# Pooling of keys and values by halving additions in one tile, in an attention and mixture-of-experts kernel

## Chip, cores and metric

One core of a Trainium2 chip runs one program. Its engines are PE (matmuls), DVE (VectorE), ACT (ScalarE), POOL (GpSimd) and SP (which issues most DMAs). The metric is the device time of one execution in microseconds; the median of the runs counts.

## The reference

Three stages follow each other. The change lies in the first. Keys and values are averaged over eight neighbouring tokens before attention.

```python
B, H, S, D = q.shape            # 8, 8, 576, 64
k_p = k.reshape(B, H, S // 8, 8, D).mean(axis=3)
v_p = v.reshape(B, H, S // 8, 8, D).mean(axis=3)
scores = np.matmul(q, k_p.transpose(0, 1, 3, 2)) / np.sqrt(D)
attn = np.exp(scores - np.max(scores, axis=-1, keepdims=True))
attn = attn / (np.sum(attn, axis=-1, keepdims=True) + 1e-09)
x = np.matmul(attn, v_p)        # then [B * S, H * D] = [4608, 512]
```

The second stage picks one of eight experts for each of the 4608 rows (gate logits plus a bias of the row's modality) and applies the expert's two matrices with a ReLU between. The third applies `w_in`, h times softmax(h), a normalization and `w_out`.

## The kernel before

**Pooling.** Of a batch, the 8 heads times 72 pooled tokens are 576 rows of 8 x 64 numbers. They are cut into five row blocks of 128, 128, 128, 120 and 72 rows (`ROWS`), so there are 40 blocks, numbered 5 b + c. A block's keys are loaded as a tile `kc` of 512 columns, its values as `vc` (`load_kv`, L263 to L271), each from five buffers. DVE sums the keys over the eight tokens by one `tensor_reduce` whose input is read with a stride of 64 (`pool_k`, L301). The values of blocks 0 to 18 (`VD`, L45) are summed by DVE in the same way (L340), those of blocks 19 to 39 by POOL in three additions of halves, through the scratch tiles `v1` and `v2` (L343 to L347). Sums go to the tile `kv`, whose part 0 is keys and part 1 values.

**Around it.** Batch 0 has a path of its own (`first_keys`, L306): five key loads, the first queries, five value loads; its value sums are held behind its last keys (L350). Groups of two, two and one blocks then pass five steps: sums (`kv_a`), transposes on PE (`kv_b`, L359), copies on ACT (`kv_e`), gate products on PE (`kv_c`, L383) and, in `kv_d`, a mask product on POOL that spreads the values over heads (L399).

**Attention.** There are 20 units, five to a pair of batches; 36 row tiles in all. A unit's queries are transposed (`st_q`), scores are made in three banks (`st_s`), their maxima found on DVE (`st_m`, L466), exponentials on ACT (`st_x`), transposed (`st_e`), multiplied with the values (`st_v`, L545) and divided on DVE (`st_w`, L568 to L576); the rows are stored by SP (L577). After each nine tiles the rows are ranked by expert (`route`, `rank`) and POOL scatters them in nine indirect DMAs (`scatter`, L640). The first slot's expert weights are loaded and split when 18 tiles are scattered.

**Order.** The lists `ORDER` and `loads` (L779) give the program order of a step. The order on PE, ACT, DVE, POOL and SP is then set by the framework's scheduler, by program order and its own estimates of when an instruction is ready; each engine works through its queue in order. SP's queue holds key, value and query loads, row stores, weight loads, and, once, the loads of the modality table and the bias (L803 to L816). A load waits in it until a buffer of its tile is free.

**After attention.** The fixed weights `w_in` and `w_out` are decoded from 64-bit words on ACT, DVE (L188 to L208) and POOL (L195 to L209) beside the first two slots. From then on 19 slots of 256 rows pass through the experts and the third stage, with PE as the busy engine.

Of the kernel before, what the change touches and what calls it, by code (L numbers as in the profile page):

```python
# [7 lines left out]
F32 = mybir.dt.float32  # L8
# [29 lines left out]
# which groups of a unit's scores have their maximum taken off on VectorE  # L38
SUBG = ((2,),) * 20
# after which of the first values the second unit's queries are loaded  # L40
# [3 lines left out]
# the row blocks (five to a batch) whose values are pooled on VectorE, not GpSimd  # L44
VD = tuple(range(19))  # L45
Q0 = 3
LKV, LQ = 3, 5
# the first slot's loads, by steps since its expert was chosen
# [10 lines left out]
# a step's parts: what, which, and how many units ahead of the step  # L59
# [9 lines left out]
# the last pair's tiles that are routed together  # L69
# [10 lines left out]
def chunk_attention_moe_solu_kernel(  # L80
# [79 lines left out]
    def fixed_load(src, n, i, *_):  # L160
        kk, cc = divmod(i, n // 512)
        # before the first slot's exponentials their place serves too
        in_ec = (i if n > 512 else 8 + i) in EC
        st = ec_p.tile([128, FF], F32, name="ec") if in_ec else stg_p.tile([128, 1024], F32, name="stg")
        rows = src[128 * kk:128 * kk + 128, 512 * cc:512 * cc + 512]
        if src.dtype != I64:
            SY.dma_start(out=st[:, 0:512], in_=rows)
        else:
            SY.dma_start(out=st.bitcast(I32), in_=rows.bitcast(I32))
        return st  # L170

    def fixed_chunk(st, src, n, i, hi, lo, scale=None):
        """Chunk i (512 columns) of a [rows, n] weight, rows 128 to a partition block, as hi + lo."""
# [4 lines left out]
        if src.dtype != I64:  # L178
            t = st[:, 0:512]
        else:  # L180
            w = st.bitcast(I32).rearrange("p (f w) -> p f w", w=2)
            w0, w1_ = w[:, :, 0], w[:, :, 1]
            ta = dec_p[0].tile([128, 512], I32, name="ta")
            tb = dec_p[0].tile([128, 512], I32, name="tb")
            t, r = ta.bitcast(F32), tb.bitcast(F32)
            # the high word read as a float32 orders magnitudes too: below float32's range they become 0
            ACT.activation(out=t, in_=w1_.bitcast(F32), func=ACTF.Abs)
            DVE.tensor_scalar(out=t, in0=t, scalar1=2.0 ** -15, scalar2=None, op0=ALU.max)  # L188
            DVE.tensor_scalar(out=ta, in0=ta, scalar1=3, scalar2=0x3FFFFFFF, op0=ALU.logical_shift_left, op1=ALU.bitwise_and)
            DVE.scalar_tensor_tensor(out=ta, in0=w1_, scalar=-0x40000000, in1=ta, op0=ALU.bitwise_and, op1=ALU.bitwise_or)  # L190
            DVE.tensor_scalar(out=tb, in0=ta, scalar1=-0x800000, scalar2=None, op0=ALU.bitwise_and)
            ACT.activation(
                out=w0.bitcast(F32), in_=w0.bitcast(U32), func=ACTF.Copy, scale=2.0 ** -52 if sc is None else g52[:, kk:kk + 1])
            ic = i if n > 512 else 8 + i
            (DVE if ic in RD else POO).tensor_tensor(out=r, in0=w0.bitcast(F32), in1=r, op=ALU.mult)  # L195
# [15 lines left out]
    def expert_load(src, e, kk, n):  # L211
        """Rows of expert e's weight for n of its row blocks of 128, 1024 floats to a partition."""
        st = stg_p.tile([128, 1024], F32, name="stg")
        SY.dma_start(
            out=st.rearrange("p (k f) -> p k f", k=n),
            in_=src[bass.ds(e, 1), 128 * kk:128 * (kk + n), :].rearrange("a (k p) f -> p (a k) f", p=128))
        return st
# [6 lines left out]
    def behind(op, other):  # L224
        """Keeps op behind an earlier one of its engine."""
        tc.add_manual_dep(op.ins, other.ins.name, mybir.DependencyInfo(mybir.DependencyClass.NoSync, mybir.DependencyReason.DATA))
# [20 lines left out]
    t1_p = att0.enter_context(tc.tile_pool(name="t1_p", side="right", bufs=BUFS["t1"]))  # L247
# [11 lines left out]
    k_t, v_t, q_t = {}, {}, {}  # L259

    KVS = ((k, k_t, "kc"), (v, v_t, "vc"))

    def load_kv(b, c, which=KVS):  # L263
        a, z = ROWS[c]
        for src, dst, nm in which:
            t = kv_p.tile([128, POOL * D], F32, name=nm)
            SY.dma_start(
                out=t[:z - a],
                in_=src[b].rearrange("h (s t) d -> (h s) (t d)", t=POOL)[a:z],
            )  # L270
            dst[b, c] = t  # L271
# [26 lines left out]
    # a batch's pooled keys and values in three groups of its five row blocks  # L298
    KG = [(b, cs) for b in range(B) for cs in ((0, 1), (2, 3), (4,))]

    def pool_k(kv, kc, n):  # L301
        DVE.tensor_reduce(out=kv[:n, 0], in_=kc[:n].rearrange("p (t d) -> p d t", d=D), axis=AX.X, op=ALU.add)
# [3 lines left out]
    def first_keys():  # L306
        """The first batch's pooled keys, ahead of its values."""
        for c in range(5):
            load_kv(0, c, KVS[:1])
        load_q(0)  # L310
        for c in range(5):
            load_kv(0, c, KVS[1:])
            if c == Q1:
                load_q(1)
        for b, cs in KG[:3]:
            a0, z0 = ROWS[cs[0]][0], ROWS[cs[-1]][1]
            kt = pstr.tile([128, 512], F32, name="tr")
            for c in cs:
                a, z = ROWS[c]
                kv = kx_p.tile([128, 2, D], F32, name="kv")  # L320
                pool_k(kv, k_t.pop((b, c)), z - a)
# [6 lines left out]
    def kv_a(i):  # L328
        b, cs = KG[i]
        kv_st[i] = []  # L330
        for c in cs:
            n = ROWS[c][1] - ROWS[c][0]
            vc = v_t.pop((b, c))
            if b == 0:
                kv = kv_0[c]
            else:
                kv = kx_p.tile([128, 2, D], F32, name="kv")
                pool_k(kv, k_t.pop((b, c)), n)
            if 5 * b + c in VD:
                op = DVE.tensor_reduce(out=kv[:n, 1], in_=vc[:n].rearrange("p (t d) -> p d t", d=D), axis=AX.X, op=ALU.add)  # L340
            else:
                op = None
                v1 = t1_p.tile([128, 4 * D], F32, name="v1")  # L343
                v2 = t1_p.tile([128, 2 * D], F32, name="v2")
                POO.tensor_tensor(out=v1[:n], in0=vc[:n, 0:256], in1=vc[:n, 256:512], op=ALU.add)
                POO.tensor_tensor(out=v2[:n], in0=v1[:n, 0:128], in1=v1[:n, 128:256], op=ALU.add)
                POO.tensor_tensor(out=kv[:n, 1], in0=v2[:n, 0:64], in1=v2[:n, 64:128], op=ALU.add)  # L347
            if b == 0 and op is not None:
                # the keys are waited for first
                behind(op, kv_last[-1])  # L350
# [52 lines left out]
    # units: five per pair of batches (b, k0) (b, k1) (the last 64 tokens of both) (b+1, k0) (b+1, k1)  # L403
# [27 lines left out]
    # scores of a unit in three banks of (up to) six blocks of 72: block i is head i//n of row r = i%n  # L431
    # (in the unit of two batches' ends: head i)
# [89 lines left out]
    def group(i):  # L522
        """The tiles that are routed together: a pair of batches' nine, of the last pair five and four."""
# [4 lines left out]
    # heads' 73 columns follow each other over two banks: seven of them end at the first one's end  # L528
    def st_v(u, r):
# [5 lines left out]
        if not ps2 and s_done.get(NU - 1) == 3 and not any(x[0] == "s" for x in ps):  # L535
            # no more scores: their banks hold every other tile of the last units
# [70 lines left out]
    def rank():  # L607
# [8 lines left out]
        # row p of tile j: earlier rows of its tile, and all of the tiles before it  # L616
# [39 lines left out]
    def pick_first(dst, val, tmp, mx):  # L656
        """dst = one-hot of the first largest of val, over the last axis of 8."""
# [6 lines left out]
    def choose():  # L664
        """The expert with most tokens so far, of 18 tiles, has more than SLOT: its first two slots go first."""
# [48 lines left out]
    def take(pool, shape, dt, name):  # L714
        """A tile: a new one, or, in the last slot's two branches, the next of those that both hold."""
# [40 lines left out]
    # the first slot's first stages go between the last units' parts  # L756
    begun = [0]

    def early(*at):
        if at and begun[0] < len(EARLY) and at != EARLY[begun[0]]:  # L760
            return
        while begun[0] < 5 and (not at or begun[0] < len(EARLY) and EARLY[begun[0]] == at):
            i = begun[0]
            begun[0] += 1
            if i == 0:
                assert min(kv_n) == len(KG) and not k_t and not v_t
# [35 lines left out]
    def more_loads():  # L802
# [14 lines left out]
        # a row's place in xs and its token  # L817
# [114 lines left out]
    def tables(tp):  # L932
# [23 lines left out]
        # the expert that goes last: the one with fewest rows in its last slot  # L956
# [35 lines left out]
        # rows left from a slot's start; its first row; its expert (an empty slot has the first one's)  # L992
# [68 lines left out]
    def st_S(s, t, pf):  # L1061
        """Off with the mean; the sum of squares."""
# [7 lines left out]
    def st_R(s, t, n):  # L1070
        """Rows' scale: r / sqrt(r^2 mean(c^2) + 1e-6) with r = 1 / (sum + 1e-9)."""
# [7 lines left out]
        # 1 / sqrt: a first value from the bits, then Newton's steps  # L1079
# [51 lines left out]
    def switch_regs(s):  # L1131
        """Whether slot s needs another expert's weights, which, and its first row."""
# [16 lines left out]
    def switch_split(ce, sts, dh, dl, n, pool=(), after=()):  # L1149
        with tc.If(ce[0] == 1):  # L1150
            for i in range(4):
                ops = expert_split(sts[i], flat(dh[:, n * i:n * i + n]), flat(dl[:, n * i:n * i + n]), POO if i in pool else DVE)
                if i == 0:
                    # behind what the tensor engine waits for
# [22 lines left out]
    for s in range(NSTAT - 1):  # L1177
# [8 lines left out]
        if s > 1:  # L1186
            # behind what the tensor engine waits for
# [209 lines left out]
```

## Time and profile before

| | |
|---|---|
| median of three runs | 1095.69 us (1093.2 to 1097.76) |
| span of the profiled execution | 1114.2 us |
| PE, DVE, ACT, POOL busy | 1060.4, 573.9, 403.9, 218.2 us |
| mean granted clock of TensorE | 0.981 |

The profiled execution is one run under the hardware profiler; its own time is known as its span, 18.5 us above the median of the runs. Shares are of the span; the stages differ, so each is read in a window of its own. PE's busy time counts modelled ends of pipelined matmuls. A line number is that of the kernel before.

### The profile page before, as it was taken

The numbers are of one execution on the slowest core, as the hardware profiler recorded it, in microseconds if no ns is written. First come the engines' busy times: TensorE is split into PE (matmuls) and PEld (weight loads), VectorE is DVE, ScalarE is ACT, GpSimd is POOL, SyncE is SP. The second block draws the span as 40 slices with busy tenths as digits, with TensorE's granted clock in tenths as the row PEclk, the third lists the DMA queues.
The fourth block names the chain that finished last, engine by engine and source line by source line (L and its number), as shares of the span: only waits on it lengthen the run. The fifth ranks groups of instructions, "written<-read, shape, count | busy, mean of one in ns | idle before, by whom it ended". The sixth has DMA issues, their size and how long they took to land.

```text
span 1114.2 us, 18506 instructions
## 1 busy us (share of the span) xinstructions
PE 1060.4 (95%) x6961; PEld 963.0 (86%) x6961; DVE 573.9 (52%) x1460; ACT 403.9 (36%) x870; POOL 218.2 (20%) x284
## 2 busy tenths in 40 slices
PE   5898979789999999999999999999999999999997
PEld 4788868788889899898998989999898998989875
DVE  7986757899953434333444433434335343333254
ACT  3666657444522322222234222322234222222232
POOL 3147453453420101101013010100121011010001
PEclk8999989989999999999999999999999999999999
DMA  9887856332200101001033010101221010010000
GB/s 254 222 243 216 242 170 213 107 115 96 77 30 11 38 1 39 29 11 39 1 115 100 15 39 2 37 8 32 97 93 39 1 39 26 8 39 2 19 19 32
DMA packets 58960, 81.19 MB, mean 73 GB/s; under 512 B 16670, under 2 KB 33054, under 8 KB 58848
## 3 DMA queue, kind: packets, MB, share of 16 engines
q1 hardware_dynamic: 50608, 59.28, 17.7%
q0 software_dynamic: 7152, 19.46, 5.1%
q10 hardware_dynamic: 1088, 1.05, 0.4%
q8 instruction: 59, 0.97, 0.4%
q14 instruction: 53, 0.43, 0.1%
HBM read 59.37 MB, written 19.63 MB: 71 GB/s over the span
## 4 chain that ended last, share of the span: by engine, by line
PE 62%; issue 10%; DVE 1%; POOL 1%; another core or an unknown queue 0%; POOLq 0%; ACT 0%
PE ab L736 15%; PE ab L735 15%; PE ab L737 15%; PE h L736 5%; PE h L735 5%; PE h L737 5%; PE tr L1101 2%; PE tr L728 1%; POOL out_dram L1120 1%; DVE ta L208 0%; DVE hl L752 0%; DVE ec L1067 0%; DVE ec L1054 0%; DVE c L1077 0%
## 5 line engine op out<-in xcount | busy, mean ns | idle before, releaser
L1120 POOL DMA_INDIRECT out_dram<-o,ids x37 | 37.7, 1019 | 683.0 <-ACT o L1119 557.9
L735 PE MATMUL ab<-hh,w2h 128*128 128x256 f32 x576 | 165.9, 288 | 3.7 <-DVE rpf L626 3.7
L737 PE MATMUL ab<-hh,w2l 128*128 128x256 f32 x576 | 163.7, 284 | 0.0
L736 PE MATMUL ab<-hl,w2h 128*128 128x256 f32 x576 | 163.2, 283 | 0.5 <-DVE hl L752 0.5
L735 PE MATMUL ab<-xh,w1h 128*128 128x256 f32 x544 | 154.6, 284 | 2.9 <-DVE hl L752 1.8
L736 PE MATMUL ab<-xl,w1h 128*128 128x256 f32 x544 | 154.3, 284 | 0.0
L737 PE MATMUL ab<-xh,w1l 128*128 128x256 f32 x544 | 153.5, 282 | 0.0
L736 PE MATMUL h<-wil,yh 128*128 128x512 f32 x296 | 116.4, 393 | 1.9 <-POOL wil L202 1.9
L735 PE MATMUL h<-wih,yh 128*128 128x512 f32 x296 | 117.9, 398 | 0.1
L737 PE MATMUL h<-wih,yl 128*128 128x512 f32 x296 | 116.0, 392 | 0.0
L735 PEld LDWEIGHTS ab<-hh,w2h 128*128 128x128 f32 x576 | 109.9, 191 | 3.8 <-issue 3.8
L736 PEld LDWEIGHTS ab<-hl,w2h 128*128 128x128 f32 x576 | 110.0, 191 | 0.7 <-DVE hl L752 0.7
L737 PEld LDWEIGHTS ab<-hh,w2l 128*128 128x128 f32 x576 | 109.1, 189 | 0.0
L1053 ACT ACTIVATE ec<-h,c,ids 128x1024 f32<-128x1024 f32 x36 | 43.4, 1207 | 177.4 <-DVE c L1052 177.3
L735 PEld LDWEIGHTS ab<-xh,w1h 128*128 128x128 f32 x544 | 102.5, 188 | 4.4 <-DVE hl L752 2.0
L737 PEld LDWEIGHTS ab<-xh,w1l 128*128 128x128 f32 x544 | 104.0, 191 | 0.0
L736 PEld LDWEIGHTS ab<-xl,w1h 128*128 128x128 f32 x544 | 102.8, 189 | 0.8
L1051 DVE TENSOR_REDUCE c<-h 128x1 f32<-128x1024 f32 x37 | 45.3, 1224 | 111.2 <-PE h L737 111.2
L735 PE MATMUL ab<-woh,ch 128*128 128x512 f32 x256 | 99.7, 389 | 0.0
L737 PE MATMUL ab<-woh,cl 128*128 128x512 f32 x256 | 99.6, 389 | 0.0
L736 PE MATMUL ab<-wol,ch 128*128 128x512 f32 x256 | 99.6, 389 | 0.0
L752 DVE SCALAR_TENSOR_TENSOR hl<-ab,hh 128x512 fp32r<-128x512 f32 x68 | 46.9, 689 | 98.2 <-ACT hh L751 98.2
(279 smaller groups left out, 2048.2 us busy)
## 6 DMA issues: line engine op xcount, KB each, us to landing
stg<-in_moe_w_dram SPq DMA_DIRECT2D x24, 512.0 KB
xs<-xr SPq DMA_DIRECT2D x36, 256.0 KB
qc<-in_q_dram SPq DMA_DIRECT2D x16, 512.0 KB
kc<-in_k_dram SPq DMA_DIRECT2D x24, 256.0 KB
vc<-in_v_dram SPq DMA_DIRECT2D x24, 256.0 KB
stg<-in_moe_w_in_dram SPq DMA_DIRECT2D x4, 512.0 KB
ec<-in_moe_w_in_dram SPq DMA_DIRECT2D x4, 512.0 KB
ec<-in_moe_w_out_dram SPq DMA_DIRECT2D x4, 512.0 KB
```

The lines of the kernel that those rows point to most:

```text
L728: PE.transpose(out=p[:, kk, :], in_=x[:, 128 * kk:128 * kk + 128], identity=ident)
L735: PE.matmul(out=o, lhsT=hi, rhs=rhi, start=first, stop=False)
L736: PE.matmul(out=o, lhsT=hi, rhs=rlo, start=False, stop=False)
L737: PE.matmul(out=o, lhsT=lo, rhs=rhi, start=False, stop=last)
L752: b = DVE.scalar_tensor_tensor(out=hl[:, m:m + 2], in0=p, scalar=0.0, in1=hh[:, m:m + 2].bitcast(F32), op0=ALU.max, op1=ALU.subtract)
L1051: DVE.tensor_reduce(out=mx[:, c1], in_=pf, axis=AX.X, op=ALU.max)
L1053: ACT.activation(out=ec, in_=pf, func=ACTF.Exp, bias=nb[:, c1], scale=g[:, c1], accum_out=s1[:, c1])
L1101: PE.transpose(out=p[:, j, :], in_=c[:, f:f + 128], identity=ident)
L1120: sc = POO.indirect_dma_start(out=out, out_offset=bass.IndirectOffsetOnAxis(ap=d["tok"][t], axis=0), in_=o, in_offset=None, bounds_check=N ...
```

## The change

Keys and values of a block get one tile `kvc` of two parts from five buffers; each part has its own load. `pooled` sums the eight tokens by three additions, in place in that tile: columns 0 to 255 plus 256 to 511, then halves of that, then halves again into `kv`. From batch 1 on the additions take both parts at once (2 x 256, 2 x 128, 2 x 64 results). They run on DVE, except in the eleven blocks 9, 12, 15, ... 39, where they run on POOL, keys included. Batch 0 does its keys and its values separately, both on DVE. The strided sums and the scratch tiles `v1`, `v2` are gone. Comments are dropped too.

```diff
-VD = tuple(range(19))
+PV = tuple(range(9, 40, 3))
...
-    t1_p = att0.enter_context(tc.tile_pool(name="t1_p", side="right", bufs=BUFS["t1"]))
...
-    def load_kv(b, c, which=KVS):
+    def load_kv(b, c, which=(0, 1)):
         a, z = ROWS[c]
-        for src, dst, nm in which:
-            t = kv_p.tile([128, POOL * D], F32, name=nm)
+        if (b, c) not in kv_t:
+            kv_t[b, c] = kv_p.tile([128, 2, POOL * D], F32, name="kvc")
+        for i in which:
             SY.dma_start(
-                out=t[:z - a],
-                in_=src[b].rearrange("h (s t) d -> (h s) (t d)", t=POOL)[a:z],
+                out=kv_t[b, c][:z - a, i],
+                in_=(k, v)[i][b].rearrange("h (s t) d -> (h s) (t d)", t=POOL)[a:z],
             )
-            dst[b, c] = t
...
-    def pool_k(kv, kc, n):
-        DVE.tensor_reduce(out=kv[:n, 0], in_=kc[:n].rearrange("p (t d) -> p d t", d=D), axis=AX.X, op=ALU.add)
+    def pooled(eng, kv, t, i, n):
+        for w in (256, 128):
+            eng.tensor_tensor(out=t[:n, i, 0:w], in0=t[:n, i, 0:w], in1=t[:n, i, w:2 * w], op=ALU.add)
+        return eng.tensor_tensor(out=kv[:n, i], in0=t[:n, i, 0:D], in1=t[:n, i, D:2 * D], op=ALU.add)
...
-                pool_k(kv, k_t.pop((b, c)), z - a)
+                pooled(DVE, kv, kv_t[b, c], slice(0, 1), z - a)
...
             if b == 0:
                 kv = kv_0[c]
+                with tc.issue_after(kv_last[-1].ins):
+                    pooled(DVE, kv, t, slice(1, 2), n)
             else:
                 kv = kx_p.tile([128, 2, D], F32, name="kv")
-                pool_k(kv, k_t.pop((b, c)), n)
-            if 5 * b + c in VD:
-                op = DVE.tensor_reduce(out=kv[:n, 1], in_=vc[:n].rearrange("p (t d) -> p d t", d=D), axis=AX.X, op=ALU.add)
-            else:
-                op = None
-                v1 = t1_p.tile([128, 4 * D], F32, name="v1")
-                v2 = t1_p.tile([128, 2 * D], F32, name="v2")
-                POO.tensor_tensor(out=v1[:n], in0=vc[:n, 0:256], in1=vc[:n, 256:512], op=ALU.add)
-                POO.tensor_tensor(out=v2[:n], in0=v1[:n, 0:128], in1=v1[:n, 128:256], op=ALU.add)
-                POO.tensor_tensor(out=kv[:n, 1], in0=v2[:n, 0:64], in1=v2[:n, 64:128], op=ALU.add)
-            if b == 0 and op is not None:
-                behind(op, kv_last[-1])
+                pooled(POO if 5 * b + c in PV else DVE, kv, t, slice(0, 2), n)
```

## Rows read from the trace of the kernel before

**Rows 1.** Windows: start:end and length in us, busy time (instructions) by engine, clock, DMA

```profile
core 0: us, PE busy (x) PEld busy (x) DVE busy (x) ACT busy (x) POOL busy (x), PEclk, DMA share, GB/s
0.00:28.00 28.00, 15.26 (x72) 11.45 (x73) 21.88 (x31) 9.17 (x26) 10.52 (x45) 0.88 0.96 253
...
28.00:84.00 56.00, 50.39 (x381) 45.16 (x380) 49.75 (x125) 37.50 (x128) 15.32 (x34) 1.00 0.84 233
84.00:196.00 112.00, 98.14 (x709) 88.30 (x708) 77.41 (x240) 73.04 (x232) 57.08 (x90) 0.92 0.70 209
196.00:308.00 112.00, 97.77 (x709) 92.81 (x708) 103.30 (x268) 51.77 (x93) 52.30 (x44) 0.94 0.30 97
308.00:1114.00 806.00, 798.84 (x5098) 725.25 (x5096) 321.56 (x799) 232.46 (x394) 82.99 (x74) 1.00 0.10 33
```

**Rows 2.** Waits of DVE, 28 to 84 us, then 84 to 196 us: total, times, longest

```profile
DVE rs L568 <- PE av L545: 4.1, 3, 1.9
...
DVE rs L568 <- PE av L545: 9.0, 10, 3.1
DVE nm L466 <- PE s L452: 7.0, 4, 3.2
DVE rs L568 <- remote: 7.0, 1, 7.0
```

**Rows 3.** The pooling instructions, by line, in ns: min/median/max, first and last start us

```profile
L302 DVE TENSOR_REDUCE kv<-kc x40: 999/1031/1054, 3.5 to 159.9; 128x64 f32<-128x512 f32 x24, 120x64 f32<-120x512 f32 x8, 72x64 f32<-72x512 f32 x8
L340 DVE TENSOR_REDUCE kv<-vc x19: 956/1025/1042, 11.4 to 66.1; 128x64 f32<-128x512 f32 x12, 120x64 f32<-120x512 f32 x4, 72x64 f32<-72x512 f32 x3
L345 POOL TENSOR_TENSOR v<-vc x21: 720/725/736, 67.7 to 155.3; 128x256 f32<-128x256 f32 x12, 72x256 f32<-72x256 f32 x5, 120x256 f32<-120x256 f32 x4
L346 POOL TENSOR_TENSOR v<-v x21: 449/455/459, 68.5 to 156.1; 128x128 f32<-128x128 f32 x12, 72x128 f32<-72x128 f32 x5, 120x128 f32<-120x128 f32 x4
L347 POOL TENSOR_TENSOR kv<-v x21: 313/318/323, 69.0 to 156.6; 128x64 f32<-128x64 f32 x12, 72x64 f32<-72x64 f32 x5, 120x64 f32<-120x64 f32 x4
L399 POOL TENSOR_TENSOR vb<-kv,mask x40: 289/402/511, 12.6 to 157.0; 128x192 f32<-128x192 f32 x16, 128x128 f32<-128x128 f32 x8, 120x128 f32<-120x128 f32 x8, 72x64 f32<-72x64 f32 x8
```

**Rows 4.** DVE instructions with two SBUF inputs, by line, in ns: min/median/max

```profile
L201 DVE TENSOR_TENSOR ta<-ta,wih x8: 677/684/694, 217.1 to 257.6; 128x512 f32<-128x512 f32 x8
L984 DVE TENSOR_TENSOR spv<-soh,t x2: 354/770/1187, 249.7 to 252.9; 128x200 f32<-128x200 f32 x2
```

**Rows 5.** DVE beside POOL: durations by line in ns, then the timeline (start, length in us)

```profile
L190 DVE SCALAR_TENSOR_TENSOR ta<-stg,ta x8: 676/686/1667, 213.7 to 303.5; 128x512 int32<-128x512 int32 x8
L202 POOL TENSOR_TENSOR wil<-ta,tb x8: 1262/1372/1749, 218.0 to 258.3; 128x512 fp32r<-128x512 f32 x8
...
223.87 1.34 POOL L202 TENSOR_TENSOR wil<-ta,tb 128x512 fp32r<-128x512 f32 x1
224.11 1.65 DVE L190 SCALAR_TENSOR_TENSOR ta<-stg,ta 128x512 int32<-128x512 int32 x1
```

**Rows 6.** Timeline, key loads on SP, the first value sums, a store of rows

```profile
8.18 2.43 SPq L267 DMA_DIRECT2D kc<-in_k_dram  x3
...
11.45 3.12 DVE L340 TENSOR_REDUCE kv<-vc 128x64 f32<-128x512 f32 x3
...
37.49 0.38 SPq L267 DMA_DIRECT2D kc<-in_k_dram  x1
...
63.37 0.57 SPq L577 DMA_DIRECT2D xs<-xr  x1
```

**Rows 7.** Timeline: the second burst of nine scatters, POOL behind it, PE's transposes

```profile
134.76 1.01 POOL L640 DMA_INDIRECT perm<-meta,rpi  x1 [6.88 <-DVE rpi L627]
...
145.88 0.74 POOL L345 TENSOR_TENSOR v<-vc 128x256 f32<-128x256 f32 x1
146.70 0.45 POOL L346 TENSOR_TENSOR v<-v 128x128 f32<-128x128 f32 x1
...
160.91 0.38 PE L359 MATMUL tr<-ident,kv 128*128 128x128 f32 x2
```

More of the change, by code (lines that the diff above doesn't have):

```diff
@@ L257, in chunk_attention_moe_solu_kernel @@
     blank(0)
-    k_t, v_t, q_t = {}, {}, {}
-    KVS = ((k, k_t, "kc"), (v, v_t, "vc"))
-    def load_kv(b, c, which=KVS):
+    kv_t, q_t = {}, {}
+    def load_kv(b, c, which=(0, 1)):
         a, z = ROWS[c]
-        for src, dst, nm in which:
-            t = kv_p.tile([128, POOL * D], F32, name=nm)
+        if (b, c) not in kv_t:
+            kv_t[b, c] = kv_p.tile([128, 2, POOL * D], F32, name="kvc")
+        for i in which:
             SY.dma_start(
-                out=t[:z - a],
-                in_=src[b].rearrange("h (s t) d -> (h s) (t d)", t=POOL)[a:z],
+                out=kv_t[b, c][:z - a, i],
+                in_=(k, v)[i][b].rearrange("h (s t) d -> (h s) (t d)", t=POOL)[a:z],
             )
-            dst[b, c] = t
     def load_q(i):
@@ L308, in first_keys @@
         for c in range(5):
-            load_kv(0, c, KVS[:1])
+            load_kv(0, c, (0,))
         load_q(0)
         for c in range(5):
-            load_kv(0, c, KVS[1:])
+            load_kv(0, c, (1,))
             if c == Q1:
@@ L332, in kv_a @@
             n = ROWS[c][1] - ROWS[c][0]
-            vc = v_t.pop((b, c))
+            t = kv_t.pop((b, c))
             if b == 0:
                 kv = kv_0[c]
+                with tc.issue_after(kv_last[-1].ins):
+                    pooled(DVE, kv, t, slice(1, 2), n)
             else:
                 kv = kx_p.tile([128, 2, D], F32, name="kv")
-                pool_k(kv, k_t.pop((b, c)), n)
-            if 5 * b + c in VD:
-                op = DVE.tensor_reduce(out=kv[:n, 1], in_=vc[:n].rearrange("p (t d) -> p d t", d=D), axis=AX.X, op=ALU.add)
-            else:
-                op = None
-                v1 = t1_p.tile([128, 4 * D], F32, name="v1")
-                v2 = t1_p.tile([128, 2 * D], F32, name="v2")
-                POO.tensor_tensor(out=v1[:n], in0=vc[:n, 0:256], in1=vc[:n, 256:512], op=ALU.add)
-                POO.tensor_tensor(out=v2[:n], in0=v1[:n, 0:128], in1=v1[:n, 128:256], op=ALU.add)
-                POO.tensor_tensor(out=kv[:n, 1], in0=v2[:n, 0:64], in1=v2[:n, 64:128], op=ALU.add)
-            if b == 0 and op is not None:
-                behind(op, kv_last[-1])
+                pooled(POO if 5 * b + c in PV else DVE, kv, t, slice(0, 2), n)
             kv_st[i].append(kv)
@@ L765, in early @@
             if i == 0:
-                assert min(kv_n) == len(KG) and not k_t and not v_t
+                assert min(kv_n) == len(KG) and not kv_t
                 att0.close()
```

## The prediction

> **What bounds the kernel now.** I read the windows first. From 308 us on PE is busy 798.84 of 806 us, and nothing in the change reaches that stretch [rows 1]: the change can only move the moment at which it begins. Before it come the first loads (0 to 28 us), attention and the decoding of the fixed weights. In the first 28 us DMA is busy 96% of the time. In 28 to 84 us DVE is busy 49.75 of 56 us and DMA 84%. In 84 to 196 us DVE is busy only 77.41 of 112. In 196 to 308 it is busy 103.30 of 112 with work that the change leaves alone, so a gain made earlier is passed on whole [rows 1]. PE's 50.39 us in 28 to 84 says less than it seems, as ends of matmuls are modelled.
>
> Then the waits of DVE. Between 28 and 84 us the largest comes to 4.1 us: there VectorE is the engine that others queue for. Between 84 and 196 us it waits 9.0 and 7.0 us for PE's matmuls, and 7.0 us at once without a named releaser, so a lighter DVE helps little there [rows 2]. The pooling instructions come third: 40 key sums of 1031 ns, 19 value sums of 1025 ns (the last at 66.1 us), and for the other 21 blocks' values three additions on POOL of 725, 455 and 316 ns [rows 3]. Blocks 0 to 18, both parts on DVE, thus lie in the DVE-bound stretch; blocks 19 to 39 mostly in the looser one.
>
> **The sum.** DVE loses 40 x 1.031 + 19 x 1.025 = 60.7 us. The new additions have two SBUF inputs, of 512, 256 and 128 columns (keys and values together), or 256, 128 and 64 for batch 0. DVE has such rows at 512 columns (684 ns) and at 200 (354) [rows 4], a slope of 1.06 ns a column: 413 ns at 256, 278 at 128, 210 at 64. A whole block costs 0.684 + 0.413 + 0.278 = 1.375 us in place of 2.06; half a block 0.90 in place of 1.03. 24 whole blocks and 10 halves are 33.0 + 9.0 = 42.0 us, so DVE is 18.7 us lighter: 39.1 - 22.8 = 16.3 us in blocks 0 to 18 (five of them by halves, ten whole, four gone to POOL), and 21.7 - 19.3 = 2.4 us in blocks 19 to 39.
>
> POOL loses 21 x 1.50 = 31.4 us. It gains 11 blocks, each of a 512-column addition (1.26 us, the least that POOL takes for that shape, [rows 5]), 0.725 and 0.455: 2.45 us, 26.9 in all. So it is no busier. But on these blocks keys now pass through POOL too.
>
> The new price is not in those durations. All of DVE's old sums ran beside POOL untouched, between 956 and 1054 ns [rows 3]. A DVE instruction with two SBUF inputs does not: L190 takes 676 ns when alone, and 1.65 us when it starts at 224.11 while POOL's addition runs from 223.87 for 1.34 us; it ends 0.55 us after that one. POOL's L202, in turn, takes between 1.26 and 1.75 us [rows 5]. They exclude each other. How often the new additions will meet POOL isn't shown; I bound it. At least 0 (the additions fall between POOL's). At most every one of POOL's eleven new chains, 26.9 us, holds DVE for its whole length, with 40 x 0.40 = 16 us of mask products on top [rows 3]. As a middle I take chance meetings: from 28 to 84 us POOL would be busy with 15.3 - 9.0 + 14.7 = 21 of 56 us (six old chains out, six new in), a share of 0.37. An addition that finds it busy waits about 0.4 us, half of a typical POOL instruction. 30 additions x 0.37 x 0.4 = 4.4 us. For the 42 additions of blocks 19 to 39, with POOL busy 26 of 90 us (21 products of 0.40 and seven chains of 2.45), it is 42 x 0.29 x 0.4 = 4.9 us. Batch 0 meets little. DVE's net is then 16.3 - 4.4 = 11.9 us lighter early, 4.9 - 2.4 = 2.5 us heavier late.
>
> The Trainium skill (SBUF — State Buffer, Who interferes with whom) states this as a rule that speaks against the change: a tensor_reduce on trn2 never contends with GpSimd, a two-input SBUF operation does, and the second to issue fully blocks. By that rule alone the sum would lie anywhere between the two bounds above; the rows on L190 agree with it.
>
> What of the early 11.9 us reaches the end? The next limit in 28 to 84 us is DMA, busy 0.84 x 56 = 47 us: the stretch can shrink by 9 at most. DVE's own waits there, 6.3 us, stay, and the loads of the modality table and bias (L803 to L816) stand in SP's queue ahead of the key load at 37.49 [rows 6] whatever DVE does; what is saved before that partly turns into a wait for keys. I take 8 us. Late, DVE has slack: of its 2.5 us, 0.5.
>
> **Edits that cost little.** One tile for both parts is freed only by the last addition of a block. Block 5's keys now load at 8.18 us, after block 0's keys are summed; they would have to wait for block 0's values, about 12 us (first value sum 11.45) [rows 6]. That is 3.8 us later for three loads. The first 2.8 MB (five blocks' keys and values of 512 columns, one tile of queries of 1024), at the 253 GB/s of the first window [rows 1], keep DMA fed until about 13 us, so I take 0.5 us, between 0 (or a gain, if SP then issues the second query first) and 3.8. Key and value loads keep their number, 80, and their queue. A POOL block's slot and keys may be stuck behind nine scatters: 134.76 to 145.88 us now, with block 35's values next on POOL [rows 7]. After the change block 36 would stand there, done by 148.3; its transpose (the 37th of 40, in the pair at 160.91, [rows 7]) comes 12 us later, so this is hidden. If it weren't, it would cost up to the burst's 11 us. Each addition needs the one before it; on POOL such a chain shows 0.08 us between instructions [rows 7]. On DVE I charge nothing, since the scheduler can put other work between; if it doesn't, 68 gaps x 0.08 = 5.4 us. The two dropped scratch tiles cost nothing.
>
> Sum: -8 + 0.5 + 0.5 = -7 us on the profiled execution, 1114.2 to 1107. The runs have a median of 1095.69, 18.5 us below that span; I carry the difference over unscaled: 1095.7 - 7 = **1088.7 us**.
>
> **Rivals.** (A) *DVE was the limit everywhere.* Meetings are rare and the loads follow: up to 18.7 us, I put 15, so 1081. For it: DVE's share before 84 us. Against: 96% DMA before 28 us, and DVE's waits on PE after 84. (B) *The loads take DVE's place.* The additions are shorter, but DVE then waits for keys behind the modality loads, or for its own chain, and gains shrink to about 2 us: 1093.5. For it: DMA at 84 to 96% until 84 us, and the SP queue's stop at 37 us. A change that doesn't do what it says, its additions no shorter in place than the sums, ends here too. (C) *Exclusion wins.* POOL and DVE work on neighbouring blocks that land together, so their chains meet regularly, not by chance. Place: DVE's additions beside POOL's blocks 9, 12, ... 39. If each chain holds DVE for its full 2.45 us, and the products hold it for none, DVE gets 26.9 - 18.7 = 8.2 us heavier, about 1104. It decides from where a DVE addition waits 18.7/102 = 0.18 us on average; my middle is 9.3/102 = 0.09. For it: L190's 1.65 us. (It is the rule of the Trainium skill cited above, carried to its end.) Against: POOL's chains fill only 26.9 of some 150 us.
>
> **How the numbers follow.** My forecast has 0.38, A 0.15, B 0.29, C 0.18. What can be told from no change is about 0.5%, 5.5 us: below 1090.2 is faster, above 1101.2 slower. Forecast and A make faster 0.53; B makes 0.29 the same; C 0.18 slower. The range, 1077 to 1101, leaves out the far end of A and more than half of C, some 2 in 10. The forecast's own range is 1084 to 1090; where the first loads cost their full 3.8 us, or DVE's chains their 5.4 us of gaps, the gain falls under 4 us, and I count that to B.
>
> **What would show it.** Right: DVE additions near 0.68, 0.41 and 0.28 us; DVE's busy time before 196 us down by 9 to 19 us; the row tiles of the first pair of batches stored earlier, the first single one before 63.37 us [rows 6], and the step into the solid PE stretch some 7 us earlier. C shows as additions of 1 us and more that end shortly behind a POOL addition. B shows as DVE waits on key loads around 37 to 45 us. I am wrong if the early stretch is shorter and the end is not, or if DVE's time falls and PE's start of the second pair stays.

## The result, and the profile after

In the first measurement the changed kernel took 1113.74 us (median of five runs, 1106.85 to 1114.49) and the kernel before 1096.95 us (five runs, 1093.2 to 1099.29): a ratio of 1.0136, interval 1.0109 to 1.0163. By the ratio it is slower by 15 us (the medians lie 16.8 us apart), where 7 us of gain were forecast.

A caution on bases first. The kernel before was met at two levels: 1097 to 1098 us in the first measurement and in those of e9 to e12 and e17, and 1115 to 1117 us in the four others (e1 to e4, e5 to e8, e13 to e16, e18). The 20 profiles fall into two kinds to match. In 14 of them VectorE or ScalarE waits before 230 us, at least once for over 1 us, for a release that the trace only calls "remote"; in the changed kernel's first profile, e9 to e12 and e17 there is no such wait. The measurements ran on several chips, but the chip alone does not decide: the one numbered 10 gave 1097.6 us beside e9 and 1115.1 us beside e18. "A chip of the first kind" or "of the second kind" stands below for a chip while it was at that level; what decides the level is not known. The profile ahead of the prediction has a span of 1114.2 us and is of the second kind. So ratios are taken against the kernel before in the same measurement, and stages are compared between the changed kernel's first profile (span 1105.1, the run of 1106.85 us, of the first kind) and a profile of the kernel before on a chip of that kind (e17, span 1097.8).

The windows of the changed kernel answer to [rows 1]; columns as there (window, length, busy time of PE, PEld, DVE, ACT, POOL with counts, clock, DMA share, GB/s):

```profile
0.00:28.00 28.00, 19.37 (x84) 15.29 (x84) 17.81 (x54) 9.98 (x29) 10.81 (x43) 0.88 0.94 247
28.00:84.00 56.00, 50.08 (x372) 44.43 (x371) 42.83 (x131) 37.35 (x128) 21.18 (x31) 1.00 0.85 236
84.00:196.00 112.00, 104.42 (x795) 95.16 (x794) 88.09 (x301) 77.25 (x245) 56.79 (x69) 0.98 0.77 224
196.00:308.00 112.00, 93.37 (x672) 87.58 (x671) 95.89 (x230) 47.36 (x81) 48.72 (x39) 0.95 0.24 82
```

The same windows of the kernel before in e17:

```profile
0.00:28.00 28.00, 18.05 (x77) 14.35 (x78) 22.57 (x33) 9.53 (x27) 10.89 (x45) 0.83 0.98 264
28.00:84.00 56.00, 51.11 (x379) 45.71 (x379) 49.63 (x125) 37.84 (x129) 15.01 (x33) 0.99 0.84 227
84.00:196.00 112.00, 105.55 (x807) 97.42 (x806) 88.89 (x288) 79.29 (x246) 63.08 (x95) 0.97 0.80 226
196.00:308.00 112.00, 99.62 (x697) 92.57 (x696) 100.96 (x235) 50.64 (x86) 48.58 (x41) 0.97 0.24 81
```

VectorE became 12.4 us lighter before 196 us (161.1 to 148.7), as the change meant. PE did not get on: 372 matmuls in place of 379 between 28 and 84 us, in the same 50 to 51 of 56 us. And behind 196 us, where the change touches nothing, PE is busy 6.2 us less. The timeline shows where the end went; attention's last row tile (xr), then the last matmul, first of the kernel before (e17):

```profile
196.82 0.69 DVE L570 TENSOR_TENSOR xr<-av,rc 128x512 f32<-128x512 f32 x1
...
1089.95 0.39 PE L737 MATMUL ab<-woh,cl 128*128 128x512 f32 x1
```

and of the changed kernel:

```profile
197.82 0.68 DVE L562 TENSOR_TENSOR xr<-av,rc 128x512 f32<-128x512 f32 x1
...
1097.45 0.39 PE L729 MATMUL ab<-woh,cl 128*128 128x512 f32 x1
```

Attention ends at the same time within 1 us (197.5, 198.5). From there to the last matmul it is 892.8 us before and 899.3 after. That stretch, "the tail" below, is the loss that these two profiles show: 6.5 of 7.3 us.

The additions themselves, by line (busy time and mean of one, then idle time before them), answer to [rows 3, 4]:

```profile
L302 DVE TENSOR_TENSOR kvc<-kvc 128x512 f32<-128x512 f32 (+7 forms) x68 | 38.4, 572 | 3.2 <-DMA kvc<-in_k_dram 2.5
L303 DVE TENSOR_TENSOR kv<-kvc 128x128 f32<-128x128 f32 (+5 forms) x34 | 9.3, 275 | 0.5
```

VectorE's 102 additions take 47.7 us, 5.7 above the 42.0 without meetings and under the middle estimate for them (9.3). Not all of the 5.7 need be meetings: the ten halves of batch 0 alone come to 9.8 us, where 9.0 were counted. The timeline of two that met POOL, which answers to [rows 5]:

```profile
100.76 1.26 POOL L302 TENSOR_TENSOR kvc<-kvc 128x512 f32<-128x512 f32 x1
101.98 0.50 POOL L391 TENSOR_TENSOR vb<-kv,mask 128x192 f32<-128x192 f32 x1
102.18 1.54 DVE L302 TENSOR_TENSOR kvc<-kvc 120x512 f32<-120x512 f32 x1
102.45 0.72 POOL L302 TENSOR_TENSOR kvc<-kvc 128x256 f32<-128x256 f32 x1
...
120.95 2.39 POOL L302 TENSOR_TENSOR kvc<-kvc 120x512 f32<-120x512 f32 x2
121.00 1.76 DVE L302 TENSOR_TENSOR kvc<-kvc 128x512 f32<-128x512 f32 x1
```

A 512-column addition, whose median here is 0.68 us, took 1.54 and 1.76 us beside POOL's. The Trainium skill (SBUF — State Buffer, Who interferes with whom) has this blocking as a rule, and the rows agree.

VectorE's longest waits between 28 and 84 us answer to the first of [rows 2]:

```profile
DVE rs L560 <- PE av L537: 5.5, 6, 2.1
DVE vb L388 <- PE tr L375: 2.7, 4, 1.7
DVE nm L458 <- PE s L448: 2.6, 2, 1.5
```

In this window VectorE waits 12.3 us for PE in all, where e17 has 5.6. Its busy time there fell by 6.8 us, its waits for PE rose by 6.7: the time that it saved it spent waiting. The single wait of 7.0 us without a named releaser, later on in [rows 2], is gone; it belongs to the other kind of chip (last section).

The first loads in SP's queue, with the store of the first single row tile, answer to [rows 6]:

```profile
12.94 1.42 SPq L277 DMA_DIRECT2D qc<-in_q_dram  x1
14.46 0.73 SPq L266 DMA_DIRECT2D kvc<-in_k_dram  x1
...
62.37 0.58 SPq L569 DMA_DIRECT2D xs<-xr  x1
```

Block 5's keys load at 14.46 us where they loaded at 8.18. Not the slot decides that: block 0's values are summed by 13.0 us. The scheduler put queries ahead of these keys, and SP's queue stood until 12.9 us for PE's transposes of the first queries:

```profile
10.94 1.97 PE L414 MATMUL tr<-ident,qc 128*128 128x128 f32 x8
```

The single store at 62.37 is 1.0 us earlier than in [rows 6], but on a chip of the same kind it is no earlier at all (62.39 in e17). The row tiles themselves end at 37.8 us (the first), 82.2 (the tenth) and 198.5 (the last), in e17 at 36.5, 81.9 and 197.5. So nothing of the early gain had arrived even by the tenth.

### The profile page after: what moved, and what is told of

Read it like the earlier page. It is cut to its first block, busy times and chain, and to the rows that moved or that the text cites. A ratio compares the mean times of both kernels' runs of the same rounds, so it can differ in the third digit from the quotient of the medians.

```text
span 1105.1 us, 18512 instructions
## 1 busy us (share of the span) xinstructions
PE 1057.0 (96%) x6961; PEld 959.7 (87%) x6961; DVE 560.6 (51%) x1503; ACT 402.8 (36%) x870; POOL 219.1 (20%) x254
```

## Experiments

Theories, as the expectations name them: **T**, the one tile holds a slot until both parts are used and loads wait; **C**, the chains of three additions cost time; **X**, VectorE and POOL shut each other out; **K**, additions queued on POOL around its bursts of nine scatters delay what stands behind them; **S**, a stop of PE at those bursts that comes and goes; **O**, the scheduler, which orders every engine's work, chose another order of the unchanged work after attention; **P**, PE is the limit early. A chain is one block's three additions.

**e1, the kernel before again** (no edit).

> The kernel before, unchanged, for a profile that stands near its usual time (the one on hand has a span of 1114 us, its runs a median of 1097). Theory S (a stall at the scatter bursts that comes and goes): the span is near 1095 and the 4.2 us in which PE, VectorE and ScalarE all stand still around 143 to 147 us are gone or shorter. If the span is near 1095 with the same stops, the 18 us of the first profile lie elsewhere.

Span 1118.4 us, on a chip where it takes 1116.6. The stop is there, PE standing for 6 us; attention ended at 218.2 us, tail 892.8. The first profile's 18 us above the timed runs are thus the difference between the two kinds.

**e2, additions alone**

```
-DVE.tensor_reduce(out=kv[:n, 0], in_=kc[:n].rearrange("p (t d) -> p d t", d=D), ...)
+halves(kv[:n, 0], kc, n)      # three additions; the values of VD likewise
```

> The kernel before with its two tiles and its division of the work (values of blocks 19 to 39 on POOL), and only VectorE's 59 strided sums as three additions each (256, 128 and 64 columns). Theory C (the chains of three additions and the order that the scheduler makes of them cost the time): most of the loss is here, 1108 to 1114 us. Theory T (one tile for both parts) and theory K (keys on POOL): no loss, 1088 to 1099. Theory X (VectorE and POOL shut each other out): VectorE's sum of additions is 59 x 0.90 = 53 us where undisturbed and 8 us or more above that where it is shut out; the time then rises by less than 5 us, to about 1101.

1120.77 us, ratio 1.0021 (0.9997 to 1.0045). Part by part the additions save little. The rows of the keys in its profile, by line,

```profile
L302 DVE TENSOR_TENSOR kc<-kc 128x256 f32<-128x256 f32 (+2 forms) x40 | 17.3, 435 | 2.4 <-DMA kc<-in_k_dram 2.4
L303 DVE TENSOR_TENSOR kc<-kc 128x128 f32<-128x128 f32 (+2 forms) x40 | 12.3, 309 | 0.3
L304 DVE TENSOR_TENSOR kv<-kc 128x64 f32<-128x64 f32 (+2 forms) x40 | 9.8, 245 | 0.7
```

come to 39.4 us in place of 40 x 1.03. C falls as the cause: there is no loss to speak of, and no gain.

**e3, one tile alone**

```
-t = kv_p.tile([128, POOL * D], F32, name=nm)      # kc and vc
+kv_t[b, c] = kv_p.tile([128, 2, POOL * D], F32, name="kvc")      # once for both
```

> The kernel before with keys and values of a row block in one tile, and its strided sums and its division of the work kept. Theory T (the slot of a block comes free only with the last use of both parts, and loads wait for it): most of the loss is here, 1106 to 1114 us. Theories C, K and X: within 4 us of the kernel before, 1093 to 1101, with the loads of block 5 a few us later.

1125.11 us, ratio 1.0073 (1.0048 to 1.0097): the merged tile alone loses as much as the whole change did on such chips (e5). But its profile put the loss in an unexpected place: attention ended at 213.1 us, and the tail was 901.0.

**e4, no block on POOL** (on the changed kernel, as are e6 to e8)

```
-PV = tuple(range(9, 40, 3))
+PV = ()
```

> The changed kernel with no block on POOL: all 40 blocks' additions on VectorE, 11 x 1.38 = 15 us more of them than in the changed kernel. Theory X (exclusion) and theory K (keys held in POOL's queue behind scatters): the loss goes, 1092 to 1101 us, and no addition of 512 columns takes over 1 us except beside the mask products. Theories C and T: VectorE is 15 us heavier and nothing is won, 1114 to 1122.

1118.73 us, ratio 1.0016 (0.9993 to 1.0038); attention ended at 206.4 us, the earliest of these four, and the tail was again long, 900.8 us. The instruction order of the three explained it. With two tiles (e1, e2) all engines have one and the same order after attention; with one tile (e3, e4, the changed kernel) they all have another, though that work is unchanged. This became theory O. Beside e5, which has the same order and eleven blocks on POOL, the ratio is 0.0044 lower: that is what X and K asked for, on this kind of chip (see e7).

**e5, the changed kernel beside its variants** (no edit).

> The changed kernel as it is, beside its variants on the same chip. Theory O (the one tile makes the scheduler choose another order of the decoding after attention, and that order is some 7 us longer): from attention's last row tile (the last xr) to the last matmul about 900 us, where the two runs with two tiles showed 893 and 894; and attention itself ends before that of the kernel before. Ratio to the kernel before 1.011 to 1.016, as at first. Theories T, X, K: the loss lies ahead of the last xr.

1123.24 us, ratio 1.006 (1.0038 to 1.0081) on a chip where the kernel before takes 1116.9. Tail 900.2 as O says. Attention ended at 214.5 us, no later than the 211.6 to 218.2 of the kernel before on such chips.

**e6, block 38 for block 39**

```
-PV = tuple(range(9, 40, 3))
+PV = tuple(range(9, 39, 3)) + (38,)
```

> The changed kernel with block 38 on POOL in place of block 39, two neighbouring blocks, the last of the 40. Up to some 150 us the order of every engine is the same; after attention VectorE, ScalarE and PE have the order of the kernel before in place of the changed one's. Theory O: 6 to 8 us faster than e5, ratio to the kernel before about 1.005 to 1.008, and 893 us from the last xr to the last matmul. Theories T, X, K and C: as e5 within 2 us, since tile, additions, loads and POOL's share stay.

1118.57 us, ratio 1.0023 (1.0005 to 1.0042), 4.7 us faster than e5, tail 894.9. Tile, additions, loads and POOL's share are those of e5: O holds, its size somewhat under the expectation.

**e7, one block on POOL**

```
-PV = tuple(range(9, 40, 3))
+PV = (38,)
```

> The changed kernel with one block on POOL, block 38; against e4 (none), whose ratio was 1.0016, it again differs in the order after attention, which is here that of the kernel before. Theory O: 7 us faster than e4, ratio 0.993 to 0.998. Otherwise: as e4, 1.000 to 1.004.

1112.21 us, ratio 0.9963 (0.994 to 0.9986): 0.4% faster than the kernel before, and 0.5% better than e4 with the other order. Tail 893.9. This is the second pair that differs by the order, apart from one block. And e7 is 0.0060 below e6, which has the same order and eleven blocks on POOL (0.0039 below e14, the same kernel as e6). So on chips of the second kind POOL's blocks do cost something, some 4 to 7 us with e4 and e5. PE's stop at the second burst goes with it: 5.85 and 5.86 us in e5 and e6, 2.31 in e4, at most 1.82 in e7.

**e8, late blocks on POOL**

```
-PV = tuple(range(9, 40, 3))
+PV = tuple(range(19,40))
```

> The changed kernel with both parts of all blocks 19 to 39 on POOL (21 chains of 2.45 us, 51 us of POOL, in place of eleven) and none of blocks 9 to 18; the order after attention is that of the kernel before. Theory X (exclusion): POOL is busy with two-input additions in the whole of 84 to 170 us, so VectorE's rows with two SBUF inputs are stretched there and attention ends 5 us or more later than in e6. Theory K: transposes wait behind scatters, with the same sign. Theory O alone: like e6, ratio about 1.005.

1117.48 us, ratio 1.0004 (0.9984 to 1.0024); attention ended at 216.4 us (e6: 219.0), tail 893.5. With 21 chains on POOL in place of eleven nothing is lost: X and K, which wanted 5 us or more, fall in that form. Going from eleven to 21 adds nothing, though e8 too is 0.0041 above e7; which chains cost something was not found.

**e9, without blocks 24 and 36 on POOL**

```
-PV = tuple(range(9, 39, 3)) + (38,)
+PV = (9, 12, 15, 18, 21, 27, 30, 33, 38)
```

> Kernel e6 without its POOL blocks 24 and 36, the two whose additions stand on POOL directly around the first and the second burst of nine scatters; their additions go to VectorE, the other nine POOL blocks stay. e6 had a ratio of 1.0023 to the kernel before, e7 (one POOL block) 0.9963, 6.7 us apart. Theory K (additions queued on POOL behind a burst delay the mask product behind them, and PE with it): most of the 6.7 us comes with these two blocks, ratio 0.997 to 0.999, and PE's stop at the second burst falls from 5.9 us to under 3. Theory X (exclusion, by the number of additions on POOL): a fifth of it, 1.000 to 1.002, and the stop stays.

1104.61 us, ratio 1.006 (1.0039 to 1.008), outside both expectations: this chip is of the first kind (before: 1097.6), where PE's stops don't occur, so there was nothing to win for K. Attention ended at 198.9 us, as in the changed kernel (198.5), and the tail is 893.3 where that has 899.3: O once more, with two POOL blocks fewer besides.

**e10, the kernel before with all values on VectorE**

```
-VD = tuple(range(19))
+VD = tuple(range(40))
```

> The kernel before with all 40 values summed on VectorE by strided sums (21 more of 1.02 us, 21.5 us of VectorE, nothing pooled on POOL), two tiles as before. Theory K: PE's stop at the second burst, 6.0 us in the kernel before, falls under 3 us although VectorE is 21 us heavier, and the time falls or stays: 0.994 to 1.000. If VectorE's load counts from 84 us on: slower by 5 us and more, 1.005 and above.

1113.88 us, ratio 1.0152 (1.0128 to 1.0177), same chip as e9. On such a chip VectorE's load does count from 84 us on: 21.5 us more of it moved attention's end from 197.5 (e17) to 213.3 us.

**e11, one addition of three** (on e7) leaves out the first two additions, so that two of every eight tokens are summed.

```
-for w in (256, 128):
-    eng.tensor_tensor(out=t[:n, i, 0:w], in0=t[:n, i, 0:w], in1=t[:n, i, w:2 * w], op=ALU.add)
```

> Kernel e7 with only the last of the three additions: the first two are left out, so that two of each eight tokens are summed. VectorE loses about 45 of its 57.6 us of additions, some 22 of them in blocks 0 to 18. Prediction's view (VectorE is the limit from 28 to 84 us, DMA the next at 9 us): attention's first 12 row tiles end 8 us or more earlier than in e7 and the time falls by 8 to 15 us, ratio 0.983 to 0.989. Theory P (PE, 50 us busy of 56 there, is the limit): at most 2 us earlier by 84 us, ratio 0.992 to 0.997.

1100.52 us, ratio 1.0025 (1.0008 to 1.0042), same chip as e9. The window of 28 to 84 us, and VectorE's longest waits in it:

```profile
28.00:84.00 56.00, 52.03 (x378) 46.45 (x378) 31.92 (x121) 35.46 (x119) 6.24 (x14) 0.94 0.86 242
...
DVE rs L558 <- PE av L535: 10.4, 9, 3.0
DVE vb L386 <- PE tr L373: 6.1, 5, 2.8
DVE nm L456 <- PE s L442: 5.6, 3, 3.2
```

VectorE is down from 49.63 to 31.92 us between 28 and 84 us, and its waits for PE are up from 5.6 to 23.5: the two together are 55.2 us in e17, 55.1 in the changed kernel and 55.4 here. PE for its part waited 1.6 us for VectorE and 1.2 for loads. From the first row tile to the tenth it took 47.5 us (30.4 to 77.9), where e17 took 45.4. So VectorE does not set the pace there, which is shown, and the waits name PE, as P has it. (That PE does 378 matmuls where it did 379 says less: its granted clock was 0.94 in this window, 0.76 from 28 to 42 us, and 0.99 in e17.) Attention ended at 189.7 us, 7.8 earlier than in e17 for 37 us less of VectorE; 6.1 of them were there at the first row tile. The tail, in the order of the kernel before, grew to 897.5. So even what is gained ahead of 196 us is not all passed on. Against both expectations the time is not below that of the kernel before at all.

**e12, mask products of blocks 33 and 34 on VectorE** (on e7)

```
+VBD = (33, 34)
...
-POO.tensor_tensor(out=vb[:n, p0:p0 + nh, 0:D], ...
+(DVE if 5 * b + c in VBD else POO).tensor_tensor(out=vb[:n, p0:p0 + nh, 0:D], ...
```

> Kernel e7 with the mask products of blocks 33 and 34, which stand on POOL behind the second burst, on VectorE (two instructions of 0.3 to 0.4 us). Theory K carried on: PE's stops at the second burst, 1.41, 1.15 and 1.82 us in e7, mostly go, and the time falls by 2 to 4 us, ratio 0.993 to 0.995. If the stops come from something else (VectorE's own chain, the scatters themselves): no change, 0.995 to 0.998.

1103.13 us, ratio 1.0047 (1.0026 to 1.0068), on the chip of e9: inconclusive, since PE doesn't stop at the bursts there. What won in e7 does not win on this kind of chip, as far as this near relative tells. Beside e9 with its nine POOL blocks (1.006) the intervals overlap: a price of POOL's blocks does not show here.

**e13, e14: the kernel before, and e6, once more**

> The kernel before once more, unchanged, for a profile on this chip. Theory S: where its runs come near 1097 us, PE does not stop for 6 us at the end of the second burst of nine scatters (142 to 148 us) nor for 4 us at the third, and attention's last row tile ends near 196 us; where they come near 1117 us, it stops at both and ends near 213 to 218. From the last row tile to the last matmul 893 us either way.

> Kernel e6 again (the changed kernel with block 38 on POOL for block 39, and with the order after attention of the kernel before). On a chip without the stops at the bursts the changed kernel had a ratio of 1.0136. Theory O: 0.006 less, 1.006 to 1.009, and what is left above 1.000 lies ahead of the last row tile. If the order after attention is nothing there: 1.011 to 1.015. On a chip with the stops: 1.002, as before.

On a chip of the second kind (1117.3). e13: 1114.19 us, stops at both bursts, attention to 211.6, tail 893.4. e14: 1117.79 us, ratio 1.0002 (0.9981 to 1.0023), tail 893.5. The changed kernel with the order after attention kept is no slower than the kernel before here, and no faster.

**e15, one tile, order kept** (e3 with block 18's values on POOL)

```
-VD = tuple(range(19))
+VD = tuple(range(18))
```

> Kernel e3 (one tile, strided sums; 1.0073 with stops) with the values of block 18 on POOL, which gives it the order after attention of the kernel before. Theory O: 6 to 7 us faster than e3, 1.000 to 1.003. Theory T (the slot held by the later of two parts, and loads behind it): the loss stays, 1.005 to 1.009.

1120.77 us, ratio 1.0039 (1.0018 to 1.006), where e3 had 1.0073; tail 893.6. About half of e3's loss was the order; the rest, some 4 us, is ahead of it and fits T: the tenth row tile ends at 90.6 us where e13, the kernel before on the same chip, has 82.8. But nothing here takes T alone.

**e16, additions alone, again**

> Kernel e2 again (two tiles, additions for VectorE's strided sums, order after attention of the kernel before; 1.0021 with stops). Theory S: on a chip without stops the same within 0.003. If the additions cost time ahead of 196 us only there, 1.005 and above.

1117.99 us, ratio 1.0008 (0.999 to 1.0027), tail 894.0. As e2: nothing lost, nothing gained. The other kind of chip was not reached with it.

**e17, e18: one more profile of each kernel**

> The kernel before unchanged, for its profile on a chip where it takes about 1097 us, should this be one. Theory S: no stop of PE of 4 us and more between 28 and 215 us, the last row tile of attention near 196 us, 893 us from there to the last matmul; the changed kernel's own profile on such a chip has its last row tile at 198.5 us. On a chip where it takes 1117 us: as e1 and e13.

> The changed kernel once more, for its profile. Where the kernel before takes about 1097 us: theory O alone gives 1098 + 7 = 1105 us of span, with 899 to 901 us behind the last row tile, as in its first profile; four of its first five runs took 1113 to 1114 us, so a span near 1112 would show where the other 7 us are, by theory S at the second or third burst. Where the kernel before takes 1117 us: as e5, near 1122 with the stops.

e17 came to a chip of the first kind: 1099.54 us, and the stages shown above. PE stops nowhere between 85 and 200 us for more than 2.2 us. e18 came to the second kind: 1125.77 us (before there: 1115.08), attention to 215.6, tail 900.6. So the 7 us between the changed kernel's profiled run and the four others of its first five stay unexplained; no profile of the changed kernel has a span near their 1112 us.

## Why the prediction was wrong

**The step that failed first: what of the early 11.9 us reaches the end.** VectorE was named as the engine that others queue for between 28 and 84 us, and 8 us were taken. The 11.9 us themselves arrived: before 84 us VectorE went from 72.2 to 60.6 us, 11.6 less. But PE was already at 50 to 51 of 56 us, and the prediction set that aside because ends of matmuls are modelled. What VectorE saved became waits for PE: with 49.6, 42.8 and 31.9 us of work it waited 5.6, 12.3 and 23.5 us for PE (e17, after, e11), and the tenth row tile of the changed kernel ended at 82.2 us for 81.9. The 8 us came to nothing. The small waits of VectorE in [rows 2] said only that VectorE seldom waited, not that others waited for it. The profile of before had the missing row, PE's waits for VectorE in the same window:

```profile
PE av L545 <- DVE lt L573: 0.8, 2, 0.6
```

These 0.8 us are all that a lighter VectorE could take off PE's waits there directly.

**The second: 196 to 308 us as "work that the change leaves alone, so a gain made earlier is passed on whole".** The work is unchanged, but a change to a few instructions moved the scheduler's order of it. Twenty profiles make two groups: 892.8 to 894.9 us from the last row tile to the last matmul with one order (14 profiles, and 897.5 in e11, whose attention ended earliest), 899.3 to 901.0 with the other (five: the changed kernel three times, e3, e4). Within each group VectorE's 180 instructions behind the last row tile come in one and the same order in every trace, but for e10, where a few are moved (894.2). From 308 us on PE is solid in both groups; the loss lies before that. And e11, with the order of before, passed on only part of its gain. Swapping block 39 for 38 on POOL changes the group and 4.7 us of the median. Between e4 and e7 it is 0.0053 in the ratio, between e3 and e15 0.0034, each with one block moved besides. What PE waits for between 196 and 310 us shows the difference; e17, and below it the changed kernel and e9, which has the order of before (total, times, longest):

```profile
PE tr L728 <- DMA x<-xs,ids: 2.5, 2, 1.9
...
PE h L736 <- POOL wil L202: 1.8, 2, 1.4
```

```profile
PE tr L720 <- DMA x<-xs,ids: 10.5, 2, 6.0
PE h L728 <- POOL wil L202: 5.5, 2, 2.9
```

```profile
PE tr L720 <- DMA x<-xs,ids: 6.3, 2, 5.6
PE h L728 <- POOL wil L202: 1.9, 1, 1.9
```

In the new order more decoding goes ahead of the routing on VectorE, the gathered rows of the next slots come later, and PE has nothing to put in their place: 11.7 us more on these two waits than in e17, and 7.8 more than in e9, partly won back on others. Not every such wait belongs to the order: the first, of 6.0 us, is there in e9 too (5.6). The next one is what sets the groups apart, 4.4 to 4.6 us in all five of the long tails and nothing above 1.0 us in the other fifteen. Why the scheduler turns to this order when the tiles merge, and back when a neighbouring block moves, was not found.

**The rest of the sum.** Exclusion (rival C) came to at most 5.7 us on VectorE, within its bounds and under the 9.3 of the middle. The half blocks' additions were priced at 0.90 us; keys took 0.99 and values 1.01 (e2, sums of the three means), so halving saves little where keys and values don't share the instructions. The first loads came 6.3 us later for block 5's keys, where 3.8 was the upper estimate, because queries went ahead of them and waited for PE; queries first had been counted as a possible gain. "Late, DVE has slack" was read from waits of 9.0 and 7.0 us [rows 2] in a profile from the other kind of chip than the times: without the stops VectorE is busy 88.89 of 112 us between 84 and 196 us, not 77.41, and e10 shows that load added there counts. POOL's blocks, block 36 behind the scatters among them, were put at nothing: on chips of the second kind eleven of them cost some 4 to 7 us (e4 and e5, e7 and e6); on those of the first no such price shows (e9, e12).

**Of the rivals**, B (gains shrink to nothing) describes attention, with PE in the place that it gave to the loads. None had the tail. The sign named as fatal, an early stretch that is shorter and an end that is not, didn't occur; the other did: VectorE's time fell and PE's progress stayed, down to the tenth row tile, the first of the second pair of batches.

**What stays open.** On chips of the first kind the changed kernel is at 1.0136, and e9, which has the order of the kernel before and nine POOL blocks for eleven, at 1.006. The order thus takes about half, if those two blocks count for little. The other half lies in attention or in run-to-run spread there; the two profiles (197.5 and 198.5 us) show only 1 us of it, and the changed kernel's is of the fastest of its five runs. So the cause of that half is open.

**A version that is a little faster** was found for one kind of chip alone: e7, with all blocks but one on VectorE, ratio 0.9963 (0.994 to 0.9986) where the kernel before takes 1117 us. It has the additions without the new order and almost without POOL's blocks. Its PE stops at the second burst for 1.41, 1.15 and 1.82 us and at the third for 1.68, where e5's stops for 5.85 and 4.38. What spares it these isn't settled: e8, with more on POOL, is no slower than e6. On the other kind its nearest relative, e12, is at 1.0047.

## What to carry to other kernels

An engine at 90% of a stretch may be the limit or merely busy. See first who waits for it, and leave out part of the work on the suspected one (as e11 does) before pricing what a saving there is worth. Where a scheduler orders the code, a local edit is also a new order of everything behind it: compare the instruction orders and the length of the untouched stages first, and take a pair of kernels that differ in the order alone. And take a profile of before whose span agrees with the times that it is to explain.

## What the runs showed of the hardware

The same kernel, with the same instruction order, ran through one place in two ways. During the second burst of scatters on POOL, in the changed kernel's first profile, ScalarE copies a transposed tile 0.04 us after PE's transposes end:

```profile
137.11 0.38 PE L495 MATMUL tr<-ident,e 128*128 128x128 f32 x2
...
137.53 0.59 ACT L508 COPY eT<-tr 128x512 f32<-128x512 f32 x1 [0.90 <-PE tr L495]
...
139.04 1.21 PE L537 MATMUL av<-vb,eT 128*64 128x146 f32 x6
```

In e5, on a chip of the second kind, the same copy comes 7.1 us after them, when the burst is over, and PE's products (139.04 there) at 148.63:

```profile
139.76 0.38 PE L495 MATMUL tr<-ident,e 128*128 128x128 f32 x2
...
144.36 0.95 POOL L632 DMA_INDIRECT perm<-meta,rpi  x1 [0.30 <-issue]
...
147.24 0.59 ACT L508 COPY eT<-tr 128x512 f32<-128x512 f32 x1 [7.84 <-remote]
...
148.63 1.81 PE L537 MATMUL av<-vb,eT 128*64 128x146 f32 x5 [5.85 <-DVE esi L669]
```

At the first of these rows e5 is 2.65 us behind the first profile, at the copy 9.71. The scatters themselves take no longer in e5 (0.95 to 1.01 us; 0.95 to 1.22 in the first profile). Every profile of the two kernels from chips of the second kind has this stop of PE (5.49 us in the first profile of before, 5.99 in e1, 5.75 in e13, 5.85 in e5, 5.83 in e18), and a smaller one at the third burst (3.44, 4.15, 4.21, 4.38, 3.01); e17 and the changed kernel's first profile have neither. In profiles of this kind the kernel before ends attention at 211.6 to 218.2 us, in e17 at 197.5: nearly the whole difference of their spans. The two stops make up 9 to 10 us of it; 4 to 5 us are there before the second burst, at the thirteenth row tile (93.0 in e17, 96.6 to 98.4 in the others). What ScalarE waits for at that copy the trace does not name, and no run tried it.
